# Weights and tokens staged otherwise around the block form of a two-layer network after masked attention

## The chip, the cores and the metric

One core of one Trainium2 chip runs the whole program. The metric is device time in microseconds of one execution; the kernel before was timed in three runs, and one more execution was recorded by the hardware profiler.

## What is computed

Attention over 8 batches, 8 heads, 576 positions and 64 columns, in which scores under the row's maximum less tau are dropped; its output x (4608 tokens by 512) goes through two layers with 2048 hidden columns between them, whose weights come in 64-bit floats.

```python
def _attn_ref(q, k, v, tau):
    scores = scale * np.matmul(q, k.transpose(0, 1, 3, 2))
    thresh = np.max(scores, axis=-1, keepdims=True) - tau
    scores = np.where(scores >= thresh, scores, -1000000000.0)
    ...
    return np.matmul(attn, v)

def _moe_ref(x, w_in, w_out, alpha):
    h = x @ w_in
    g = np.maximum(h, 0.0) + alpha * np.minimum(h, 0.0)
    return g @ w_out
```

## The kernel before

A number goes into TensorE as two parts, a rounded one (`hi`, `xh`, `gh`) and the rest (`lo`, `xl`, `gl`), and each product is three matmuls. The rounded part is made by ScalarE (`split_hi`, line 857), the rest by VectorE or GpSimd (`split_lo`, line 860).

The program has four parts in time. First, attention, 32 pairs of heads, with the two layers for seven of sixteen columns of weights (`fcs1`) worked in between for the first groups of 256 tokens (`groups1`). Second, what is left of that plain form: the loop over `jobs` (line 1094), here four groups of 256 tokens. For each, `first_layer` makes 12 matmuls for each of seven columns of weights, and `second_layer` two accumulators of 21 matmuls each, whose result goes to `part` in memory. The second layer of a group comes after the first one or more columns of the next group. Below, this part is called J. Third, the block form for the eight columns in `fcs2` (and one odd column, `odd`): a 2 by 2 block product is worked with seven products of sums of blocks instead of eight. Its first layer (A) takes the tokens in six blocks `s` of 768, each with four pairs of columns (`NP`), so 24 units `u`, each with seven products (`product_a`, six matmuls of 384 columns) and for two units in four an odd product (`odd_a`, twelve). Fourth, its second layer (B), nine units of 512 tokens, to which `part` is added.

Everything on TensorE, ScalarE, VectorE and GpSimd stands in the order in which it is written; only the order of transfers on SP is left to the compiler. The writing goes by cycles: `cycle()` (line 954) runs the functions that are due, those entered with `first_at_cycle` ahead of those entered with `at_cycle`, and then counts `i` up. In J a cycle is one column of the first layer, or a piece of the second one: `second_layer` calls `cycle()` after its third and its fifth column of weights and at the end of an accumulator, so three for an accumulator and six for a group. In A a cycle is one product, in B a third of one. An instruction that waits holds all that is written behind it on its engine.

Words of weights. The 64-bit words are made into 32-bit floats in seven steps (`Split64`): load, size (two ScalarE instructions), clamp, shift, sign, power, rest, and a sum (`done`). `word_at` (line 844) enters the steps at offsets that `EARLY` or `LATE` give. In J, `first_word` enters one word each `FW` = 5 cycles from cycle `i + 5` on, with its load 4 cycles ahead, into one of two raw tiles `w0`; clamp, shift, sign and power are VectorE's there, rest and `done` GpSimd's. After each second word, `sums_at` makes the seven sums of blocks and splits them. The odd column's word follows (`odd_word`). In A, `late_word` does the same for the second layer's weights, one each 14 cycles; its clamp and rest are GpSimd's, and `done` is VectorE's.

x for the block form. `x_at(s)` (line 1112) loads the four blocks of x for 768 tokens into `xr00`, `xr11`, `xr01`, `xr10`, one tile each, makes the differences and sums 7, 6, 5, 4 (`sub7`, `add6`, `sub5`, `sub4`), some of them in place, and splits the seven operands and the odd one into eleven tiles that turn (`XB`). For `s` = 0 all of it is written around the last second layer of J: load, difference 7, operand 1 and sum 6 ahead of it, the other operands (`others`) behind it and ahead of the first product. For the later blocks it is entered at cycles counted back from the first product that needs it: the load 33 before, difference 7 at 25 before, operand 1's copy at 28 before, and so on.

Accumulators. A has seven banks: X (three buffers), W and Y (two each). Products 1, 7 and 2 begin a bank; 6, 5, 3 and 4 add to one that has been saved in between. `after_a`, entered for the cycle after the product, evicts: ScalarE saves products 1, 7 and 6 as `c` (line 1306), VectorE makes the sums (line 1329), ScalarE copies them (line 1314), VectorE takes the larger with alpha (line 1317), and SP writes them to `gd`.

Of the kernel before, what the change touches and what calls it, by code (L numbers as in the profile page):

```python
# [21 lines left out]
P = 128  # L22
# [3 lines left out]
F1 = 7  # L26
# [54 lines left out]
def tile_masked_attention_moe(  # L81
# [760 lines left out]
    EARLY, LATE = (0, 1, 2, 3, 4, 5, 6), (0, 1, 3, 4, 5, 6, 9)  # L842
# [20 lines left out]
    def fetch_x(t0, n, c, lead, name):  # L863

        st = {"xr": {}}

        def load(k):
            xr = st["xr"][k] = mem.lx.tile([P, G1], F32, tag="xr", name=f"xr{name}_{k}", bufs=NCC)
            t = t0
            while t < t0 + n:  # L870
                b, o = divmod(t, S)
                m = min(S - o, t0 + n - t)
                nc.sync.dma_start(xr[:, t - t0 : t - t0 + m], xs[b][k, :, o : o + m])
                t += m

        def split(k):
            if k == 0:
                st["parts"] = tuple(mem.lx.tile([P, NCC, G1], F32R, tag=t, name=f"{t}{name}", bufs=2) for t in ("xh", "xl"))
            xr, (xh, xl) = st["xr"][k], st["parts"]
            nc.scalar.activation(xh[:, k, :n], xr[:, :n], AF.Copy)  # L880
            nc.gpsimd.tensor_tensor(xl[:, k, :n], xr[:, :n], f(xh[:, k, :n]), op=ALU.subtract)
# [8 lines left out]
    with tc.manual_schedule(engines=ENGINES) if ENGINES else ExitStack():  # L890
# [60 lines left out]
        mem.ws = pool(1, "ws", "left")  # L951
# [15 lines left out]
        def first_word(n, c):  # L967

            pr, r = divmod(n, 2)
            w = Split64(mem.ws, ("w0", 2), mem.ws, ("w1", 2), "vpp", *src_i(fcs2[n]))  # L970

            def done(w):
                if r == 0:
                    w32[pr] = mem.lx.tile([P, 2, DM], F32, tag="w32", name=f"w32_{pr}", bufs=2)
# [6 lines left out]
        def sums_at(c, pr):  # L981
# [5 lines left out]
            def temps():  # L987
                for n in (7, 6):
                    st[n] = mem.ws.tile([P, m], F32, tag=f"sum{n}", name=f"sum{n}_{pr}", bufs=1)
# [28 lines left out]
        def odd_word(io, c, lead):  # L1018
            w = Split64(mem.ws, ("w0", 2), mem.ws, ("w1", 2), "vpp", *(src_i if io == "i" else src_o)(odd))
            decode_at(c, mem.wa, w, odd, io, c - lead, io == "o")  # L1020
# [26 lines left out]
        odd_word("i", c, 4)  # L1047
# [45 lines left out]
        pending = None  # L1093
        for num, job in enumerate(jobs):
            fetch(num + 1)
            final = num == len(jobs) - 1
            for k, j in enumerate(job.todo):
                if k == 0 and num == 1 and pending.begun:
                    cycle()
# [515 lines left out]
```

## Time and profile before

| | us |
|---|---|
| median of 3 runs | 1389.84 (1389.79 to 1391.35) |
| the profiled execution | 1391.04 |
| its span, first to last instruction | 1389.26 |
| TensorE busy | 1314.6 |
| VectorE busy | 1128.8 |
| ScalarE busy | 957.3 |
| GpSimd busy | 795.8 |

The busy times are unions of instructions' spans over the whole program; the span is cut into stretches further down, since what holds TensorE differs from one to the next. A wait is shown as the engine, the tile that it was about to write and the line, and behind the arrow the instruction whose end let it go. Times in the chain of waits are its own pieces; "issue" is time for which the profile shows no wait.

### The profile page before, as it was taken

How to read it: one execution, taken by the hardware profiler on the slowest of the kernel's cores; microseconds unless marked ns; L12 is line 12 of the kernel's file. 1: busy time of each engine (PE TensorE's matmuls, PEld its weight loads, DVE VectorE, ACT ScalarE, POOL GpSimd, SP SyncE). 2: the span in 40 equal slices, each digit the busy share in tenths (PEclk: the TensorE clock that was granted, in tenths of full speed). 3: DMA queues.
4: the chain of work that ended last, by engine and by line, in shares of the span. 5: the costliest groups of instructions: out<-in, count | busy, mean ns of one | idle time of the engine just before them, and what ended most of it. 6: DMA issues, size and time to landing. Idle time of an engine off the chain costs nothing.

```text
span 1389.3 us, 26361 instructions
## 1 busy us (share of the span) xinstructions
PE 1314.6 (95%) x9052; PEld 1227.5 (88%) x9052; DVE 1128.8 (81%) x2134; ACT 957.3 (69%) x2103; POOL 795.8 (57%) x961
## 2 busy tenths in 40 slices
PE   5998899999999999999999999986999999999998
PEld 4556789999999999999999998876999998999998
DVE  6999988888888888898898864883877867878685
ACT  6888888888888888888888853444666666332332
POOL 4786675666666666676676546777877765000000
PEclk9999999999999999999999999998999999999999
DMA  8554634545545545454454313333555536756652
GB/s 250 157 152 111 181 106 125 161 117 141 149 114 152 137 132 140 132 147 122 130 160 126 104 48 116 93 99 120 173 173 173 163 116 215 239 177 188 184 153 90
DMA packets 138005, 200.35 MB, mean 144 GB/s; under 512 B 15792, under 2 KB 83408, under 8 KB 137872
## 3 DMA queue, kind: packets, MB, share of 16 engines
q1 hardware_dynamic: 137872, 198.67, 48.6%
q8 instruction: 72, 1.18, 0.4%
q14 instruction: 61, 0.50, 0.1%
HBM read 106.77 MB, written 49.69 MB: 113 GB/s over the span
## 4 chain that ended last, share of the span: by engine, by line
PE 62%; DVE 12%; DMA 8%; ACT 7%; issue 5%; POOL 5%; SPq 1%; DVEq 0%; ACTq 0%; POOLq 0%
PE av L579 11%; PE s L432 11%; PE acca L254 9%; PE pha L218 9%; PE t L476 7%; PE pX L1256 4%; PE pX L1502 3%; PE pW L1256 2%; DMA pin<-part 2%; DMA out_dram<-pin 2%; DVE gl L861 2%; DVE pin L1524 1%; DVE p L467 1%; DMA xr<-xs 1%; DVE nmx L447 1%
## 5 line engine op out<-in xcount | busy, mean ns | idle before, releaser
L447 DVE TENSOR_REDUCE nmx<-s 128x1 f32<-128x576 f32 x288 | 217.2, 754 | 72.3 <-PE s L432 69.0
L467 DVE SCALAR_TENSOR_TENSOR p<-s,thr,p 128x576 f32<-128x576 f32 x256 | 206.8, 808 | 3.0 <-ACT thr L460 2.6
L455 ACT ACTIVATE p<-s,nmx 128x576 f32<-128x576 f32 x256 | 189.9, 742 | 8.3 <-DVE nmx L447 7.9
L254 PE MATMUL acca<-wo,ga 128*128 128x512 f32 x588 | 186.3, 423 | 1.5 <-issue 0.8
L432 PE MATMUL s<-kh,qst 128*128 128x288 f32 x640 | 141.6, 311 | 34.7 <-DVE p L467 19.5
L218 PE MATMUL pha<-xh,wi 128*128 128x256 f32 x784 | 156.8, 283 | 0.2 <-ACT pra L231 0.2
L476 PE MATMUL t<-ident,p 128*128 128x128 f32 x1024 | 154.8, 274 | 0.0
L432 PEld LDWEIGHTS s<-kh,qst 128*128 128x128 f32 x640 | 100.5, 191 | 59.4 <-issue 26.3
L432 PE MATMUL s<-kl,qst 128*128 128x288 f32 x640 | 133.3, 298 | 0.0
L218 PEld LDWEIGHTS pha<-xh,wi 128*128 128x128 f32 x784 | 127.7, 190 | 4.8 <-ACT pra L231 1.5
L1256 PE MATMUL pX<-xh,wa 128*128 128x384 f32 x384 | 110.3, 345 | 18.2 <-ACT c L1306 10.2
L476 PEld LDWEIGHTS t<-ident,p 128*128 128x128 f32 x1024 | 126.7, 142 | 0.1
L254 PEld LDWEIGHTS acca<-wo,ga 128*128 128x128 f32 x588 | 101.9, 191 | 13.7 <-issue 1.2
L241 POOL TENSOR_TENSOR pta<-pta,pra 128x256 f32<-128x256 f32 x94 | 69.5, 739 | 74.0 <-ACT pra L231 71.3
L218 PE MATMUL pha<-xl,wi 128*128 128x256 f32 x392 | 110.4, 282 | 0.0
L579 PE MATMUL av<-eo,vst 128*128 128x322 f32 (+1 forms) x512 | 107.3, 333 | 0.0
L1502 PE MATMUL pX<-wb,gh 128*128 128x256 f32 x576 | 104.2, 282 | 0.0
L532 DVE TENSOR_TENSOR eo<-t,eo 128x512 fp32r<-128x512 f32 (+1 forms) x168 | 97.4, 592 | 8.2 <-ACT eo L528 8.0
L432 PEld LDWEIGHTS s<-kl,qst 128*128 128x128 f32 x640 | 102.1, 191 | 0.0
L1256 PEld LDWEIGHTS pX<-xh,wa 128*128 128x128 f32 x384 | 71.9, 192 | 21.3 <-ACT c L1306 11.6
L1502 PEld LDWEIGHTS pX<-wb,gh 128*128 128x128 f32 x576 | 89.1, 190 | 0.0
L528 ACT ACTIVATE eo<-t 128x512 fp32r<-128x512 f32 (+1 forms) x168 | 84.7, 521 | 5.3 <-PE t L476 4.4
(246 smaller groups left out, 3907.4 us busy)
## 6 DMA issues: line engine op xcount, KB each, us to landing
gd<-c SPq DMA_DIRECT2D x72, 192.0 KB
gr<-gd SPq DMA_DIRECT2D x24, 512.0 KB
kr<-in_k_dram SPq DMA_DIRECT2D x31, 320.0 KB
rb<-rvd SPq DMA_DIRECT2D x64, 144.0 KB
xs<-xa SPq DMA_DIRECT2D x32, 288.0 KB
pin<-part SPq DMA_DIRECT2D x18, 512.0 KB
out_dram<-pin SPq DMA_DIRECT2D x18, 512.0 KB
vr<-in_v_dram SPq DMA_DIRECT2D x28, 320.0 KB
```

The costliest lines, as they stand in the source:

```text
L218: nc.tensor.matmul(ph[:, :n], w[:, c, :], xx[:, c, :n], start=(c == 0 and ti == 0), stop=(c == NCC - 1 and ti == 2),)
L254: nc.tensor.matmul(acc[:m, :], gg[:, g, o : o + m], w, start=(first and ti == 0), stop=(last and ti == 2))
L432: nc.tensor.matmul(ps[:, h, :288], w, kk[:, a + h * 288 : a + (h + 1) * 288], start=(ki == 0 and i == 0), stop=(ki == 1 and i == n - 1),)
L447: nc.vector.tensor_reduce(self.nmx[:, j : j + 1], self.S[u][0][:, :, :288], axis=AX.XY, op=ALU.max, negate=True)
L455: nc.scalar.activation(pj, ps[:, :, :288], AF.Exp, bias=nmx[:, j : j + 1], scale=1.0)
L467: nc.vector.scalar_tensor_tensor(pj, ps[:, :, :288], thr[:, j : j + 1], pj, op0=ALU.is_ge, op1=ALU.mult, accum_out=self.sm[:, c : c + 1])
L476: nc.tensor.transpose(tb[:, c, :], pt[:, j, j * D + c * P : j * D + (c + 1) * P], ident)
L528: nc.scalar.activation(dst[0], ps, AF.Copy)
L532: nc.vector.tensor_tensor(dst[1], ps, f(dst[0]), op=ALU.subtract)
L579: nc.tensor.matmul(pa[:m, :n], w, x, start=(part == 0 and c == 0), stop=(part == z.parts[-1] and c == NKC))
L1256: nc.tensor.matmul(ph[:, :H1], a, x[:, c], start=(fresh and c == 0 and ti == 0), stop=(c == 1 and ti == 2), skip_group_check=not fresh,)
L1502: nc.tensor.matmul(acc[:, tb * H2 : (tb + 1) * H2], g[:, pr, tb * P : (tb + 1) * P], w, start=(fresh and n == 0 and ti == 0), stop=(n == l ...
```

## The change

It does six things.

1. Words of weights in J go through three raw tiles and three temporary ones in place of two, with the load 8 cycles ahead (not before the present cycle), and begin one cycle earlier. Their tiles lie in the pool `lx`; the late words' tiles lie in `xe`, the odd column's late weights in `br`.
2. x of a group in J is loaded into the tile of its rest and split in place; odd groups lie in `lx`, even ones in `mp1`, one tile pair each.
3. `second_layer` calls `cycle()` after its first column of weights as well: four for an accumulator, eight for a group.
4. x of the block form's first 768 tokens is loaded into a pool of its own (`xr`) as the last group of J begins; products 1 and 7 and sum 6 are written ahead of the last second layer (`some`), the other operands behind it in another order, and more of its rests are VectorE's. Half of each block's raw x has two tiles.
5. Steps of x in A move by a few cycles (load 29 before in place of 33, operand 1's copy 22 before in place of 28), late words come each 15 cycles from `begin + 6`, and their steps are spread wider.
6. Evictions, copies and the larger of two are entered with `first_at_cycle` in place of `at_cycle`.

```diff
-    EARLY, LATE = (0, 1, 2, 3, 4, 5, 6), (0, 1, 3, 4, 5, 6, 9)
+    EARLY, LATE = (0, 1, 2, 3, 4, 5, 6), (0, 1, 4, 7, 9, 10, 13)
...
-    def fetch_x(t0, n, c, lead, name):
+    def fetch_x(t0, n, c, lead, name, home):
...
-                nc.sync.dma_start(xr[:, t - t0 : t - t0 + m], xs[b][k, :, o : o + m])
+                nc.sync.dma_start(xl[:, k, t - t0 : t - t0 + m], xs[b][k, :, o : o + m])
...
-            w = Split64(mem.ws, ("w0", 2), mem.ws, ("w1", 2), "vpp", *src_i(fcs2[n]))
+            w = Split64(mem.lx, ("w0", 3), mem.lx, ("w1", 3), "vpp", *src_i(fcs2[n]))
...
-            word_at(c, w, c - 4, done)
+            word_at(c, w, max(i, c - 8), done)
...
-                job.x = fetch_x(job.t0, job.n, i, 4, job.name)
+                job.x = fetch_x(job.t0, job.n, i, 4, job.name, mem.lx if num % 2 else mem.mp1)
...
-        c = i + 5
+        c = i + 4
...
-        odd_word("i", c, 4)
+        odd_word("i", c, 8)
...
-                    if j in (2, 4):
+                    if j in (0, 2, 4):
                         cycle()
...
-                    r = st[j, k] = mem.xr.tile([P, 2, H1], F32, tag=f"xr{j}{k}", name=f"xr{s}_{j}{k}")
+                    r = st[j, k] = mem.xr.tile([P, 2, H1], F32, tag=f"xr{j}{k}", name=f"xr{s}_{j}{k}", bufs=1 + k)
...
-                home = mem.pa if slot < 7 else mem.xr if slot == 9 else mem.xe
+                home = mem.pa if slot < 7 else mem.xf if slot < 9 else mem.xe
...
-                if first and n in (7, 6, 2):
+                if first and n in (1, 7, 2, 6, 4):
                     split_lo(nc.vector, xl, st[src(n)], xh)
...
+            def some():
+                sub7()
+                hi(1)
+                lo(1)
+                hi(7)
+                lo(7)
+                add6()
+
+            def others(puts):
+                for n in (2, "o", 6, 4, 5, 3):
+                    if n == "o":
+                        hi_odd()
+                    else:
+                        if n == 4:
+                            sub4()
+                        if n == 5:
+                            sub5()
+                        hi(n)
+                    lo(n)
+                    if puts:
+                        puts.pop(0)()
+
+            if first:
+                load()
+                return some, others
-            at_cycle(max(i, need[1] - 33), load)
-            for c, fn in ((-25, sub7), (-21, add6), (-13, sub5), (-11, sub4)):
+            at_cycle(max(i, need[1] - 29), load)
+            for c, fn in ((-24, sub7), (-18, add6), (-11, sub5), (-10, sub4)):
                 at_cycle(need[1] + c, fn)
-            for c, n in zip((-27, -22, -18, -15, -4, -2, 0), USE):
+            for c, n in zip((-21, -19, -14, -12, -4, -2, 0), USE):
                 at_cycle(need[1] + c - 1, hi, n)
                 at_cycle(need[1] + c, lo, n)
...
+            if final:
+                xs0 = x_at(0)
...
         left[2].close()
-        mem.xr = pool(2, "xraw", "left")
-        others = x_at(0)
-        puts = second_layer(jobs[-1], mem.ws)
+        mem.xe = pool(2, "xe", "left")
+        some, others = xs0
+        some()
+        puts = second_layer(jobs[-1], mem.xe)
...
-                at_cycle(i + 1, copy, g, whole)
-                at_cycle(i + 2, larger, g, whole, alpha_sb)
+                first_at_cycle(i + 1, lambda: copy(g, whole))
+                first_at_cycle(i + 2, lambda: larger(g, whole, alpha_sb))
...
-            word_at(c, w, c - 8, done, fc, LATE)
+            word_at(c, w, max(i, c - 8), done, fc, LATE)
...
-            late_word(n, begin + 8 + 14 * n)
-        odd_word("o", begin + 8 + 14 * NJ, 8)
+            late_word(n, begin + 6 + 15 * n)
+        odd_word("o", begin + 6 + 15 * NJ, 8)
...
-            at_cycle(i + 1, after_a if u < NA else after_b, u, prod)
+            first_at_cycle(i + 1, lambda u=u, prod=prod: (after_a if u < NA else after_b)(u, prod))
```

## Rows read from the trace of the kernel before

**Rows 1.** Page, part 1: busy us, share of the span, instructions of TensorE.
```profile
PE 1314.6 (95%) x9052; PEld 1227.5 (88%) x9052; DVE 1128.8 (81%) x2134; ACT 957.3 (69%) x2103; POOL 795.8 (57%) x961
```

**Rows 2.** Busy time by stretch: J, start, A, turn, second layer.
```profile
core 0: us, PE busy (x) PEld busy (x) DVE busy (x) ACT busy (x) POOL busy (x), PEclk, DMA share, GB/s
850.27:945.12 94.85, 85.14 (x506) 75.41 (x505) 70.69 (x122) 42.72 (x99) 73.49 (x79) 0.95 0.35 108
945.12:976.00 30.88, 20.81 (x103) 19.84 (x102) 13.82 (x21) 15.19 (x26) 20.76 (x20) 0.83 0.34 107
976.00:1156.50 180.50, 173.89 (x980) 172.48 (x979) 135.21 (x207) 116.03 (x219) 133.26 (x120) 0.98 0.53 172
1156.50:1176.00 19.50, 16.55 (x98) 15.26 (x97) 14.48 (x24) 12.54 (x31) 12.92 (x14) 1.00 0.39 133
1176.00:1389.30 213.30, 205.82 (x1706) 203.72 (x1704) 162.99 (x179) 68.41 (x73) 1.81 (x2) 1.00 0.55 174
```

**Rows 3.** Stretches within J: two second layers, ten first layers, three first layers.
```profile
860.34:874.08 13.74, 11.43 (x44) 9.00 (x43) 8.15 (x14) 6.09 (x17) 11.89 (x14) 0.88 0.47 141
885.83:895.69 9.86, 9.86 (x44) 7.81 (x43) 7.09 (x14) 4.33 (x11) 7.33 (x9) 1.00 0.19 56
895.69:918.62 22.93, 17.05 (x122) 16.23 (x121) 20.08 (x33) 10.62 (x26) 17.72 (x21) 0.91 0.22 69
929.48:933.74 4.26, 4.26 (x37) 4.26 (x36) 4.26 (x9) 2.94 (x8) 2.36 (x3) 1.00 0.43 137
```

**Rows 4.** TensorE's waits in J: releaser, us in total, times, longest.
```profile
PE phj L218 <- DVE ptj L237: 5.8, 3, 2.5
PE accj L254 <- POOL gj L248: 3.8, 2, 2.3
```

**Rows 5.** TensorE's longest wait in the start.
```profile
PE pX L1256 <- ACT c L1306: 9.1, 2, 7.3
```

**Rows 6.** TensorE's longest wait in A.
```profile
PE pX L1256 <- DVE pZ L1329: 5.6, 3, 2.9
```

**Rows 7.** VectorE in J by group: busy, mean ns, idle before, releaser.
```profile
L236 DVE TENSOR_SCALAR ptj<-phj,alpha_sb 128x256 f32<-128x256 f32 x28 | 13.3, 476 | 3.9 <-POOL gj L248 3.7
L237 DVE SCALAR_TENSOR_TENSOR ptj<-phj,ptj 128x256 f32<-128x256 f32 x28 | 11.9, 424 | 1.0
L143 DVE TENSOR_SCALAR wti<-wti 128x512 f32<-128x512 f32 x9 | 8.4, 928 | 13.8 <-ACT wti L139 13.7
L994 DVE TENSOR_TENSOR sum<-w,sum 128x256 f32<-128x256 f32 x4 | 1.7, 426 | 0.1
```

**Rows 8.** SP's waits in J, the longest in total.
```profile
SPq L129 <- POOL w L975: 24.2, 6, 6.3
```

**Rows 9.** The shift step of words: ns min/median/max.
```profile
L146 DVE TENSOR_SCALAR wti<-wti x16: 416/582/1425, 13.6 to 929.6; 128x512 int32<-128x512 int32 x16
```

**Rows 10.** Chain of waits in the start: start us, us, what.
```profile
946.42 2.69 DVE xl L861 x3
...
956.80 4.01 DMA xr<-xs
...
961.89 1.00 POOL xt L1135
...
962.92 0.84 ACT xh L858
963.76 0.48 ACT c L1306
```

**Rows 11.** Chain of waits in A.
```profile
1029.01 5.54 DMA xr<-xs
...
1037.21 1.89 POOL wto L143
...
1048.33 2.08 PE pX L1256 x12
```

**Rows 12.** VectorE's waits in A for the late words' clamp.
```profile
DVE wto L146 <- POOL wto L143: 7.7, 4, 4.6
```

More of the change, by code (lines that the diff above doesn't have):

```diff
@@ L861, in split_lo @@
         eng.tensor_tensor(dst, src, f(hi), op=ALU.subtract)
-    def fetch_x(t0, n, c, lead, name):
-        st = {"xr": {}}
+    def fetch_x(t0, n, c, lead, name, home):
+        st = {}
         def load(k):
-            xr = st["xr"][k] = mem.lx.tile([P, G1], F32, tag="xr", name=f"xr{name}_{k}", bufs=NCC)
+            if k == 0:
+                st["parts"] = tuple(home.tile([P, NCC, G1], F32R, tag=t, name=f"{t}{name}", bufs=1) for t in ("xh", "xl"))
+            xl = f(st["parts"][1])
             t = t0
@@ L872, in load @@
                 m = min(S - o, t0 + n - t)
-                nc.sync.dma_start(xr[:, t - t0 : t - t0 + m], xs[b][k, :, o : o + m])
+                nc.sync.dma_start(xl[:, k, t - t0 : t - t0 + m], xs[b][k, :, o : o + m])
                 t += m
         def split(k):
[L877 to L881, printed above, removed]
+            xh, xl = st["parts"]
+            nc.scalar.activation(xh[:, k, :n], f(xl[:, k, :n]), AF.Copy)
+            nc.gpsimd.tensor_tensor(xl[:, k, :n], f(xl[:, k, :n]), f(xh[:, k, :n]), op=ALU.subtract)
             if k == NCC - 1:
@@ L950, in tile_masked_attention_moe @@
         mem.wa = pool(0, "wa", "left")
-        mem.ws = pool(1, "ws", "left")
+        mem.xr = pool(1, "xraw", "left")
         mem.lx = pool(2, "lx", "left")
@@ L988, in temps @@
                 for n in (7, 6):
-                    st[n] = mem.ws.tile([P, m], F32, tag=f"sum{n}", name=f"sum{n}_{pr}", bufs=1)
+                    st[n] = mem.lx.tile([P, m], F32, tag=f"sum{n}", name=f"sum{n}_{pr}", bufs=1)
                 st[5], st[3] = blk(1, 0), blk(0, 1)
@@ L1091, in second_layer @@
             return puts
[L1093 to L1099, printed above, removed]
-                    second_layer(pending, mem.mp1)
-                first_layer(job, j)
-                if k == (GB - F1 - 1 if final else 0) and num > 0 and not (num == 1 and pending.begun):
-                    second_layer(pending, mem.mp1)
-            if not final:
-                pending = job
+        start = {}
         xop = {}
@@ L1137, in temp @@
             def temp(n):
-                st[n] = mem.xr.tile([P, 2, H1], F32, tag="xt", name=f"xt{s}_{n}", bufs=2)
+                st[n] = mem.xe.tile([P, 2, H1], F32, tag="xt", name=f"xt{s}_{n}", bufs=2)
                 return st[n]
@@ L1204, in x_at @@
             at_cycle(need[1] - 16, lo, "o")
+        pending = None
+        for num, job in enumerate(jobs):
+            fetch(num + 1)
+            final = num == len(jobs) - 1
+            if final:
+                xs0 = x_at(0)
+            for k, j in enumerate(job.todo):
+                if k == 0 and num == 1 and pending.begun:
+                    cycle()
+                    second_layer(pending, mem.mp1)
+                first_layer(job, j)
+                if k == (GB - F1 - 1 if final else 0) and num > 0 and not (num == 1 and pending.begun):
+                    second_layer(pending, mem.mp1)
+            if not final:
+                pending = job
         left[2].close()
-        mem.xr = pool(2, "xraw", "left")
-        others = x_at(0)
-        puts = second_layer(jobs[-1], mem.ws)
+        mem.xe = pool(2, "xe", "left")
+        some, others = xs0
+        some()
+        puts = second_layer(jobs[-1], mem.xe)
         p1.close()
-        mem.xe = pool(6, "xe", "left")
+        mem.xf = pool(6, "xf", "left")
         mem.br = pool(3, "br", "right")
@@ L1214, in tile_masked_attention_moe @@
         others(puts)
-        start = {}
         steps = []
```

30 lines of the change are left out of this document (11 added, 19 removed).

## Prediction

> **What bounds the kernel now.** I read the page's first part first: TensorE is busy for 95% of the span [rows 1]. That is no proof that it is full, because a matmul's record overlaps the next one's. So I looked next at stretches of time, and compared what TensorE was given with what the same matmuls take where nothing holds them. The reader should see in [rows 2] five stretches: the last four groups of the plain two-layer form (J), the first 31 us of the block form (start), the rest of its first layer (A), the turn to its second layer, and the second layer.
>
> Undisturbed prices: 36 matmuls of 256 columns in 4.26 us and 42 of 512 columns in 9.86 us [rows 3], so 0.118 and 0.235 each; 12 of 384 columns in 2.08 us [rows 11], so 0.173.
> - J holds 4 x 7 x 12 = 336 of the first kind and 4 x 2 x 21 = 168 of the second: 39.7 + 39.4 = 79.1 us, and takes 94.85 [rows 2]. Lost: 15.7.
> - Start: 103 x 0.173 = 17.8 of 30.9. Lost: 13.0, with the granted clock at 0.83.
> - A: 980 x 0.173 = 169.9 of 180.5. Lost: 10.6.
> - Turn: 74 x 0.173 + 24 x 0.118 = 15.6 of 19.5. Lost: 3.9.
>
> The other engines are full in none of them: in J VectorE is busy 70.7 and GpSimd 73.5 of 94.85 us. It is order, not quantity, that costs: each engine takes its instructions in the order written, and what TensorE needs stands behind something that waits.
>
> Who holds it: in J the activation on VectorE (5.8 us) and the rests of the activations on GpSimd (3.8) [rows 4]; at the start ScalarE's eviction `c`, 9.1 us in two waits [rows 5]; in A VectorE's sum in `pZ` [rows 6]. One step further back, in J VectorE waits 13.8 us for words of weights [rows 7], whose loads wait 24.2 us for GpSimd to free one of the two raw tiles [rows 8].
>
> **Part 1, the words of weights in J.** Three raw tiles and a lead of eight cycles: word n takes the tile of word n-3, which is finished at cycle 5(n-3)+6, nine cycles before word n starts; the load at minus eight finds it free. So SP's 24.2 us of waits should go, and of VectorE's 13.8 us all but the first word (the longest, before any word has landed; its load moves one cycle only). Nothing is added: the same loads, the same steps.
>
> What is late next is VectorE itself. Its two activation steps take 13.3 + 11.9 us for 28 columns of weights [rows 7], 0.90 each. The ten groups of word and sum steps (the two rows of [rows 7] with the smallest and largest sums and eight between) add up to 48.1 us over the 46 cycles in which words run, 1.05 a cycle. A second layer now has eight cycles, not six, so the words end some five cycles sooner and nearly fall out of the last second layers, but they meet TensorE more densely. In eight first layers in a row VectorE has 8 x (0.90 + 1.05) = 15.6 us of work against TensorE's 11.4: 4.2 behind. In the second layer after it: 8 x 1.05 = 8.4 against 9.9: 1.5 caught up. In the ten after that: 19.5 against 14.2: 5.3 more. Four accumulators of slack cover 4 x 1.42 = 5.7, and a second layer needs its last activation only after 6 x 0.70 = 4.2 us. So I expect waits of 3.5 us at the first second layer (13.74 us now, 3.9 over the undisturbed 9.86 [rows 3]; GpSimd's queue there holds the same work in nearly the same order), 2 at the second, 1 to 2 in the run of ten first layers (22.93 us now for 14.2 of work [rows 3]), and none later. New loss 7.5 instead of 15.7: gain 8. Bounds: 12 if only the first wait stays, 0 if VectorE and GpSimd are as slow as at their slowest.
>
> On that last bound, a row and a rule. The row: the same shift step L146 took from 416 to 1425 ns [rows 9]. The Trainium skill (Perfetto Trace Analysis, Optimizing Scalar/DVE Operations) says that GpSimd and VectorE share a read port of SBUF, which some VectorE instructions hold alone, so that work moved between these two may not help. By that rule the denser words would lengthen each other, and two rests of x moved from GpSimd to VectorE would bring nothing; the time would be that of rival 1. The spread in the row agrees with it, but does not say by how much.
>
> **Part 2, x of the first tokens, and the start.** Now the chain is [rows 10]: three rests of 0.90 on VectorE in a row at 946.4, after the last second layer; then at 956.8 the load of the second block's x, which waited for the first block's tiles; it lands 4.0 us later; two GpSimd differences; ScalarE's `xh` at 962.9; and only then its eviction `c` at 963.8, for which TensorE stood 7.3 us. With the change the first block's loads are issued before the last group's first layers, into a pool of their own, and products 1 and 7 (difference, two copies, two rests, one sum) are prepared under the last second layer, 9.86 us of TensorE that hides about 2 x 0.84 + 4 x 0.90 = 5.3 us. The second block's x has second tiles for half of it, and its first copy stands eight steps behind the begin instead of two.
>
> What stays: products 2, 6, 4, 5, 3 and the odd one are still written ahead of the first eviction. On ScalarE and VectorE by turns, after the end of the last second layer: one copy of an accumulator, four copies of x (5 x 0.84, counting the first at the nearest row's price), four rests and differences (4 x 0.90), then the eviction 0.48: 8.3 us. TensorE reaches the step that overwrites that bank after three steps and a double one, 5 x 1.04 = 5.2 us. It waits 3.1; with something for a slower clock I take 4. The second block's first tile can be loaded once the first block's last difference is done (about 6 us in), lands 4 us later at 10, and its copy comes with the ninth step, at about 12: no wait. New loss 4 instead of 13.0: gain 9; bounds 6 (one more wait of the 3 us kind) and 12 (no wait at all).
>
> **Part 3, the steps in A.** The chain is [rows 11]: a load of x issued at 1029.0, because its tile was read until then, lands 5.5 us later; GpSimd's difference follows, behind it the late word's clamp, 1.89; behind that VectorE's shift, sign and power, with the evictions behind them; TensorE stands. VectorE waited 7.7 us for the clamp in four places, 4.6 at most [rows 12]. New: every load finds its tile free, 29 steps ahead, and the difference comes 5 x 1.04 = 5.2 us behind it, against a landing of 5.5; the shift stands three cycles behind the clamp, not two, sign, power and rest further apart; evictions are put first in their cycle. Words come every 15 cycles, half a block of 30 steps, so each block has the same pattern. On GpSimd, the difference in two halves of 1.00 [rows 10] plus the clamp of 1.89 is 3.9 us, some 4 cycles, so the shift may wait up to 1.4 us in a block, which VectorE's slack mostly takes. New loss 1.5 of 10.6: gain 9; bounds 3 (the wait comes back in each block at a third of its size) and 10.6.
>
> Third raw tile, homes of tiles, the odd word's weights in another pool: no work added. In the second layer the evictions change place in their cycle, but the rests there fall into another cycle than the sums, so I count 0. The turn's 3.9 lie in steps that the change doesn't touch; what can move there is the order of transfers, which isn't written by hand: 0, with 3 either way.
>
> **Sum.** 8 + 9 + 9 = 26 us. The profiled execution took 1391.04 (span 1389.26 and what lies around it), 1.2 above the median 1389.84; from the median: 1364.
>
> **Rivals.**
> 1. VectorE and GpSimd become the bound of J and the 8 us stay lost: 1372. For it: VectorE's 20.08 of 22.93 us in the run of ten [rows 3], and the spread in [rows 9]. Against: 13.8 us of VectorE's idle time there is plain waiting for words.
> 2. The loads don't come earlier, because SP's order stays as it is: then only the order of evictions and the x of products 1 and 7 help: about 8 us, 1382. For it: SP issues in one queue, and its waits show in [rows 8]. Against: those waits name the tile, which is now free.
> 3. All of the three losses go: 15.7 + 13.0 + 10.6 less 1 or 2, 1352.
> 4. Slower: the words locked to the block's period meet the clamp wait at every one of eight late words. At 4.4 us of TensorE each, near the longest wait of [rows 12], that is 35 instead of 10.6: 24 lost against 17 won in J and at the start, 1397. It decides from (10.6 + 17) / 8 = 3.4 us a word.
>
> **Chances.** Forecast 0.50 (1357 to 1371); rival 1 0.20; rival 2 0.09; rival 3 0.10; within 0.2% (2.8 us, about what a measurement of this kernel can tell from no change) 0.05; rival 4 0.06. Leaving out rival 2, no change and rival 4 (0.20) gives 1351 to 1380. Faster 0.89, same 0.05, slower 0.06.
>
> **What would show it.** J at about 87 us, with no wait of VectorE for word loads after the first; the waits that remain at its first two second layers. At the start one wait of ScalarE's eviction of 3 to 4 us, none of 7. In A no wait of TensorE for `pZ` above 1 us, and the shift's waits under 1.5. Wrong if J stays above 92 us, if the second block's copy still blocks ScalarE, or if one stall of A repeats in each block.

## The result, and the profile of the changed kernel

The changed kernel takes 1375.41 us (median of four, three of them from 1375.05 to 1375.66), beside 1390.59 for the kernel before on the same chip: ratio 0.9889, 95% interval 0.9870 to 0.9909. It is faster by 15 us where 26 were forecast, and nearer to rival 1 (1372) than to the forecast (1364).

The fourth took 1442.12 us at a granted clock of 0.85, is left out of the ratio, and is the one that was profiled with the result, so the profile shown is that of a further execution (1373.14 us, beside 1393.57 for the kernel before). Its windows, in the same stretches as [rows 2] (J, start, A, turn, second layer; columns are time, then busy us of each engine with its instructions, granted clock, DMA share, GB/s):

```profile
core 0: us, PE busy (x) PEld busy (x) DVE busy (x) ACT busy (x) POOL busy (x), PEclk, DMA share, GB/s
850.27:947.22 96.95, 84.96 (x505) 75.28 (x504) 72.12 (x125) 42.28 (x99) 71.27 (x77) 0.95 0.36 117
947.22:969.88 22.66, 19.72 (x104) 19.39 (x103) 13.46 (x19) 14.14 (x24) 15.06 (x14) 0.92 0.43 133
969.88:1141.67 171.79, 170.42 (x981) 170.10 (x981) 133.22 (x208) 117.17 (x219) 138.48 (x124) 1.00 0.55 178
1141.67:1158.52 16.85, 15.79 (x100) 15.45 (x99) 14.07 (x23) 13.13 (x31) 12.38 (x13) 1.00 0.40 135
1158.52:1371.00 212.48, 204.72 (x1701) 202.85 (x1699) 162.78 (x179) 68.48 (x72) 2.33 (x2) 1.00 0.55 174
```

The stretches are cut here at the same matmuls in both traces: J, then 103 matmuls of the block form, then 980, then 98. From the length of each I take the undisturbed prices of the prediction (the turn's 98 matmuls, cut so, are 69 of 384 columns and 29 of 256); what is left is lost. (Cut so, the kernel before loses 13.3, 11.0 and 4.2 in start, A and turn; by the round windows of [rows 2] it was 13.0, 10.6 and 3.9.)

| lost, us | before | forecast | after | gained |
|---|---|---|---|---|
| J | 15.7 | 7.5 | 17.8 | -2.1 |
| start | 13.3 | 4 | 4.8 | 8.5 |
| A | 11.0 | 1.5 | 2.0 | 9.0 |
| turn | 4.2 | 3.9 | 1.5 | 2.7 |

The sum is 18.1; the two profiled executions differ by 1391.04 - 1373.14 = 17.9. So the block form did what was forecast and the turn a little more. J, where 8 us were to be won, got 2 us worse. The rest of this document is about J above all.

TensorE's waits in J, which answer to [rows 4] (releaser, us in total, times, longest):

```profile
PE phj L218 <- DVE ptj L237: 8.3, 4, 3.7
PE accj L254 <- ACT gj L245: 1.9, 1, 1.9
PE accj L254 <- POOL gj L248: 1.6, 2, 1.3
```

It is still VectorE's activation that TensorE waits for, 8.3 us instead of 5.8. The three rows add up to 11.8 of the 17.8 us lost. Most of the rest is matmuls that took longer than their undisturbed price where the granted clock was lower, above all in the eight first layers from 872.33:

```profile
872.33:890.28 17.95, 14.28 (x97) 14.08 (x96) 15.54 (x26) 7.71 (x19) 13.26 (x14) 0.81 0.21 67
```

Undisturbed they take 96 x 0.118 = 11.4 us; TensorE waited 3.7 in them, and the 2.9 that are left go with the clock of 0.81.

VectorE's own waits in J, first in the kernel before, then in the changed one:

```profile
DVE wti L143 <- ACT wti L139: 13.7, 4, 7.7
DVE ptj L236 <- POOL gj L248: 3.7, 3, 2.0
DVE sum L993 <- POOL w L975: 3.2, 2, 2.0
...
DVE w L1006 <- POOL wa L861: 2.0, 2, 1.3
```

```profile
DVE sum L993 <- POOL w L975: 11.4, 4, 4.3
DVE wti L143 <- ACT wti L139: 7.8, 2, 7.3
DVE ptj L236 <- POOL gj L248: 5.3, 4, 2.0
DVE ptj L236 <- PE phj L218: 1.0, 2, 0.5
```

The loads' share fell as forecast, from 13.7 to 7.8, of which 7.3 is the first word's (5.1 of them before J begins, in both kernels). But the waits for GpSimd rose from 3.7 + 3.2 + 2.0 = 8.9 to 11.4 + 5.3 = 16.7. That VectorE's work and its waits fill J says nothing yet, since an engine that takes its instructions in order does one or the other nearly all the time. What says more is for whom it waits: for TensorE's accumulators only 1.0 us in the changed kernel, and in the kernel before no such row stands. VectorE runs behind TensorE in J, so what stands ahead of an activation in its queue can make TensorE wait.

A piece of VectorE's queue (start us, us, line, operation, idle time before it and releaser) shows how TensorE comes to stand. TensorE began eight first layers at 872.3; VectorE's first activation for them comes at 880.85:

```profile
864.57 0.42 DVE L237 SCALAR_TENSOR_TENSOR ptj<-phj,ptj 128x256 f32<-128x256 f32 x1
864.91 0.77 DVE L156 TENSOR_SCALAR wri<-wti 128x512 int32<-128x512 int32 x1
866.10 0.45 DVE L143 TENSOR_SCALAR wti<-wti 128x512 f32<-128x512 f32 x1 [0.42 <-ACT wti L139]
869.56 0.94 DVE L993 TENSOR_TENSOR sum<-w 128x256 f32<-128x256 f32 x1 [3.01 <-POOL w L975]
...
872.70 0.96 DVE L861 TENSOR_TENSOR wa<-sum,wa 128x256 fp32r<-128x256 f32 x1
873.58 0.96 DVE L1005 TENSOR_TENSOR w<-w 128x256 f32<-128x256 f32 x1
874.46 0.96 DVE L1006 TENSOR_TENSOR w<-w,sum 128x256 f32<-128x256 f32 x1
...
877.12 1.26 DVE L143 TENSOR_SCALAR wti<-wti 128x512 f32<-128x512 f32 x1
878.41 0.83 DVE L146 TENSOR_SCALAR wti<-wti 128x512 int32<-128x512 int32 x1
879.27 1.65 DVE L151 SCALAR_TENSOR_TENSOR wti<-wri,wti 128x512 int32<-128x512 int32 x1
880.85 0.47 DVE L236 TENSOR_SCALAR ptj<-phj,alpha_sb 128x256 f32<-128x256 f32 x1
```

Two things are to be seen. A 3.0 us wait for GpSimd's finished word stands ahead of thirteen steps of words. And these steps are long: the same line L1005 that takes 0.96 here takes 0.41 elsewhere. From 869.56 to 880.85 they fill 11.3 us; at the shortest record of each kind (0.42 and 0.68) it would be 6.0.

### The profile page after: what moved, and what is told of

Same layout as the page of the kernel before. It is cut to its first block, busy times and chain, and to the rows that moved or that the text cites. A ratio compares the mean times of both kernels' runs of the same rounds, so it can differ in the third digit from the quotient of the medians.

```text
span 1440.3 us, 26338 instructions
## 1 busy us (share of the span) xinstructions
PE 1393.4 (97%) x9052; PEld 1299.2 (90%) x9052; DVE 1131.6 (79%) x2136; ACT 961.3 (67%) x2103; POOL 793.5 (55%) x957
## 5 line engine op out<-in xcount | busy, mean ns | idle before, releaser
L254 PE MATMUL acca<-wo,ga 128*128 128x512 f32 x588 | 200.2, 449 | 0.1
L432 PE MATMUL s<-kh,qst 128*128 128x288 f32 x640 | 146.9, 321 | 29.4 <-DVE p L467 14.9
L476 PE MATMUL t<-ident,p 128*128 128x128 f32 x1024 | 169.8, 293 | 0.0
L218 PE MATMUL pha<-xh,wi 128*128 128x256 f32 x784 | 164.7, 293 | 0.1
L432 PE MATMUL s<-kl,qst 128*128 128x288 f32 x640 | 139.2, 309 | 0.0
L476 PEld LDWEIGHTS t<-ident,p 128*128 128x128 f32 x1024 | 135.2, 146 | 0.3
L254 PEld LDWEIGHTS acca<-wo,ga 128*128 128x128 f32 x588 | 105.7, 196 | 16.1 <-POOL ga L248 0.5
L579 PE MATMUL av<-eo,vst 128*128 128x322 f32 (+1 forms) x512 | 114.9, 350 | 0.0
L1514 PE MATMUL pX<-wb,gh 128*128 128x256 f32 x576 | 109.2, 291 | 0.0
L858 ACT ACTIVATE gh<-gr 128x1024 fp32r<-128x1024 f32 x45 | 47.6, 1058 | 75.0 <-PE pX L1514 31.6
L579 PEld LDWEIGHTS av<-eo,vst 128*128 128x128 f32 (+1 forms) x512 | 82.7, 187 | 10.3 <-issue 6.9
```

The costliest lines, as they stand in the source:

```text
L218: nc.tensor.matmul(ph[:, :n], w[:, c, :], xx[:, c, :n], start=(c == 0 and ti == 0), stop=(c == NCC - 1 and ti == 2),)
L254: nc.tensor.matmul(acc[:m, :], gg[:, g, o : o + m], w, start=(first and ti == 0), stop=(last and ti == 2))
L432: nc.tensor.matmul(ps[:, h, :288], w, kk[:, a + h * 288 : a + (h + 1) * 288], start=(ki == 0 and i == 0), stop=(ki == 1 and i == n - 1),)
L476: nc.tensor.transpose(tb[:, c, :], pt[:, j, j * D + c * P : j * D + (c + 1) * P], ident)
L579: nc.tensor.matmul(pa[:m, :n], w, x, start=(part == 0 and c == 0), stop=(part == z.parts[-1] and c == NKC))
L1514: nc.tensor.matmul(acc[:, tb * H2 : (tb + 1) * H2], g[:, pr, tb * P : (tb + 1) * P], w, start=(fresh and n == 0 and ti == 0), stop=(n == l ...
```

## The experiments

All edits are made to the changed kernel; the ratio is always against the kernel before. First the numbers of all of them, since the readings below compare them. "Lengthening" is worked out from the records: every VectorE instruction of words and sums in J, less the shortest that its kind takes (0.41 to 0.43 us; 0.68 for the lines L151, L849 and L975). In the changed kernel it is 9 x (1.017 - 0.682) for L151, 9 x (0.750 - 0.427) for L143, and so on for nine groups. Each loss in J is that of one execution, and executions of one kernel differ by up to 6.6 us (words_each_six, 1370.53 to 1377.14), so a difference of 1 to 3 us between two losses doesn't tell two kernels apart.

| kernel | ratio, 95% interval | J lost | VectorE's waits for loads | for GpSimd | lengthening |
|---|---|---|---|---|---|
| before | 1 | 15.7 | 13.7 | 8.9 | 18.9 |
| changed | 0.9889 (0.9870 to 0.9909) | 17.8 | 7.8 | 16.7 | 18.0 |
| sums_later | 0.9877 (0.9856 to 0.9897) | 18.8 | 7.6 | 19.4 | 16.5 |
| six_cycles | 0.9854 (0.9834 to 0.9874) | 16.3 | 9.1 | 16.1 | 17.7 |
| two_tiles | 0.9873 (0.9854 to 0.9891) | 20.5 | 14.7 | 12.0 | 18.3 |
| words_each_six | 0.9870 (0.9846 to 0.9893) | 19.2 | 7.8 | 15.7 | 15.2 |
| pool_light | 0.980, one run (1364.12 of 1391.69 us) | 7.0 | 10.2 | 1.8 | 13.3 |
| vector_light | 0.980, one run (1364.20 of 1391.69 us) | 9.2 | 9.9 | 20.0 | 12.4 |
| rest_on_vector | 0.9858 (0.9839 to 0.9877) | 14.9 | 6.6 | 11.5 | 17.5 |
| words_on_vector | 0.9809 (0.9794 to 0.9825) | 8.7 | 6.7 | 0 | 11.2 |
| rest_back | 0.9837 (0.9818 to 0.9856) | 16.6 | 7.6 | 7.3 | 15.0 |

**The changed kernel once more.** This is the execution shown above.

> The changed kernel as it is, for a trace at the full granted clock: the profile that came with the result shows TensorE at 0.85 of its clock. Forecast by its terms: J 7.5 us over its undisturbed price, the start 4, A 1.5, the turn 3.9; the measured 1375.4 leaves some 11 us of the forecast's 26 to be found in one of these four or in the second layer. Rival 1 expects them in J (15 lost there), rival 4 in A (a stall of the same kind in each block), an unnamed one at the turn.

**The sums later.** Theory 1 puts J's loss down to the hand-over of the finished word from GpSimd's `done` to VectorE's sums.

```diff
-                sums_at(c + 7, pr)
+                sums_at(c + 9, pr)
...
-            at_cycle(c + 2, later_sums)
+            at_cycle(c + 1, later_sums)
             for n in (5, 3):
-                at_cycle(c + 3, hi, n)
-                at_cycle(c + 4, lo, n, nc.gpsimd if n == 5 else nc.vector)
+                at_cycle(c + 1, hi, n)
+                at_cycle(c + 2, lo, n, nc.gpsimd if n == 5 else nc.vector)
```

> The sums of a pair of words in J begin two cycles later (nine after the odd word's size in place of seven) and are packed into three cycles, so that their last reads stay where they are. Theory 1, the handoff: in J the first sum on VectorE stands one cycle behind GpSimd's sum of two halves of a word (done) and waited 11.4 us for it in four places, with the activations that TensorE needs behind it; then that wait falls under 4 us, J's loss falls from 17.8 to 10 to 12 us and the time by 6 to 8, to about 1368. Theory 2, the density: VectorE and GpSimd have too much to do for TensorE's time while words run; then J loses 16 to 19 as before and other waits take the place.

The wait named went down and two others came up in its place:

```profile
DVE ptj L236 <- POOL gj L248: 7.9, 8, 2.0
DVE wti L143 <- ACT wti L139: 7.6, 2, 7.2
DVE w L1006 <- POOL wa L861: 6.1, 3, 2.0
DVE sum L993 <- POOL w L975: 5.4, 2, 4.2
```

J lost 18.8. The single hand-over isn't the cause; theory 1 falls.

**Six cycles for a second layer, and words every six cycles.** Theory 2 is the density of word steps as such: fewer in a second layer, or fewer everywhere.

```diff
-                    if j in (0, 2, 4):
+                    if j in (2, 4):
```

> The second layer of J calls the cycle three times for an accumulator again, not four; the rest of the change stays. Theory 2 (density): words meet TensorE as thinly as before, with their loads early; J's loss falls from 17.8 to 8 to 11 us, time 1366 to 1368. Theory 1 (handoff): the cycles of a second layer get longer again (1.6 us for 1.2), so the wait of the first sum falls by a half at most; J loses 12 to 15, time about 1371. If neither matters, 17 to 18 and 1375.

```diff
-    FW = 5
+    FW = 6
```

> Words of weights in J each six cycles in place of five, so that they take 55 of J's 61 cycles from its first column on. Theory 2 (density): VectorE's 1.05 us of word work for a cycle falls to 0.88, J loses 8 to 11 us, time 1366 to 1369. Theory 1 (handoff): the first sum stands as close behind GpSimd as now, and waits nearly as long; J loses 14 to 16, time 1372 to 1374.

J lost 16.3 and 19.2. With six cycles the loss moved from the eight first layers (6.6 to 2.2) into a later second layer (none to 3.9); with every sixth cycle the last second layer, free before, lost 6.9. Thinning moves the place. Theory 2, which expected a loss of 8 to 11, isn't borne out. Still, with six cycles the median is 1371.90 and the ratio 0.9854, its interval just touching the changed kernel's: the eight cycles may themselves cost some 3 us. TensorE's waits in J were no shorter for it, 5.4 + 4.3 + 2.5 = 12.2 us against 11.8; the granted clock was 0.98 over J where the changed kernel had 0.95.

**Two raw tiles again.** Part 1 undone by itself.

```diff
-            w = Split64(mem.lx, ("w0", 3), mem.lx, ("w1", 3), "vpp", *src_i(fcs2[n]))
+            w = Split64(mem.lx, ("w0", 2), mem.lx, ("w1", 2), "vpp", *src_i(fcs2[n]))
...
-            word_at(c, w, max(i, c - 8), done)
+            word_at(c, w, c - 4, done)
```

(and the same for the odd column's word)

> Words of weights in J go through two raw and two temporary tiles again, loads four cycles ahead; the rest of the change stays. The forecast's part 1 has these loads as the cause of 6 of VectorE's 13.8 us of waits before: then the wait for the words' first step comes back by 4 to 6 us, J loses 20 to 23 and the time is 1377 to 1380. Theory 1 and 2 both hold that the loads were hidden behind the same queues: J loses 17 to 19, time 1374 to 1376.

The waits for loads came back in full, 14.7 us, and the waits for GpSimd fell by 4.7. J lost 2.7 more, in an execution that was the longest of four (1378.22, median 1374.52) and had a granted clock of 0.91 over J; the ratio is the changed kernel's within the intervals. So the third tile does what it says, and it buys almost nothing: VectorE waits elsewhere instead.

**One engine made lighter.** Theory 3: GpSimd's queue is what J waits for. Rival 2': VectorE's own steps.

```diff
         def rest():
+            if fc is None:
+                return
...
-                nc.gpsimd.tensor_tensor(w32[pr][:, r], f(w.t), f(w.low), op=ALU.add)
+                nc.scalar.activation(w32[pr][:, r], f(w.t), AF.Copy)
```

> From the changed kernel, the words of J are lightened on GpSimd: the multiplication of the low part by the power (`rest`, 8 x 1.18 us) is left out, and the addition that finishes a word (`done`, 8 x 1.36 us) is replaced by a plain copy on ScalarE (8 x about 0.8 us). That takes about 20 us off GpSimd's 70 in J; the words' value is not the reference's, since their low part is left out. Theory 3 (GpSimd's in-order queue is what J waits for, first through the finished word, then through the remainder of the activations): J's loss falls from 17.8 to 6 or less, VectorE's wait of the sums for the finished word (11.4) goes, its wait of the activations for GpSimd (5.3) goes too; the time falls by about 10 us. Rival 2' (VectorE's own steps of words are too much for J): little changes, loss 12 or more.

```diff
         for d, step in zip(pace[1:], (w.clamp, w.shift, w.sign, w.power, rest)):
-            at_cycle(c + d, step)
+            if fc is not None or step in (w.clamp, rest):
+                at_cycle(c + d, step)
```

> From the changed kernel, shift, sign and power of the words in J are left out (8 x (0.56 + 1.02 + 0.75) = 18.6 us of VectorE's 71.5 in J); the words' exponents are not decoded, so their value is not the reference's. GpSimd's work stays as it is. Theory 3: J's loss stays at 12 or more, since GpSimd's queue is unchanged. Rival 2' (VectorE's own steps): the loss falls to 6 or less and the time by about 10 us.

Both took some 9 us off the time, so neither theory holds alone. VectorE's waits with the lighter VectorE (its lines stand one further down than in the changed kernel):

```profile
DVE ptj L236 <- POOL gj L248: 10.0, 7, 2.7
DVE wti L143 <- ACT wti L139: 9.9, 3, 7.4
DVE sum L994 <- POOL w L976: 9.4, 4, 5.0
```

Its waits for GpSimd even rose to 20.0 us (these two rows and one of 0.6), and still J lost only 9.2. So a wait of VectorE for GpSimd isn't a loss by itself; it becomes one when it and the work around it make an activation late for TensorE. Work of VectorE and waits for GpSimd are links of one chain, and a shorter link of either kind shortens it.

**One step moved.** If the chain is one, a step moved from the slower engine to the other should help a little.

```diff
-            w = Split64(mem.lx, ("w0", 3), mem.lx, ("w1", 3), "vpp", *src_i(fcs2[n]))
+            w = Split64(mem.lx, ("w0", 3), mem.lx, ("w1", 3), "vvp", *src_i(fcs2[n]))
```

> From the changed kernel, one step of each word in J (the multiplication of the low part, `rest`) moves from GpSimd (8 x 1.18 us) to VectorE (8 x about 0.9 us); everything is computed. Theory 3: J's loss falls from 17.8 to about 10, time 5 to 7 us below the changed kernel's. Rival 2': VectorE, the bound, gets 7 us more, so the loss rises by 3 to 7 and the time with it. If the two engines hold each other up by a shared port: no change.

J's loss fell by 2.8, in the direction of theory 3 and by less than half of what it expected; the interval (0.9839 to 0.9877) overlaps the changed kernel's.

**All steps moved.** Theories 4 and 5 differ here in sign: is it VectorE's amount of work, or the length that each instruction takes beside GpSimd's?

```diff
-            w = Split64(mem.lx, ("w0", 3), mem.lx, ("w1", 3), "vpp", *src_i(fcs2[n]))
+            w = Split64(mem.lx, ("w0", 3), mem.lx, ("w1", 3), "vvp", *src_i(fcs2[n]))
...
-                nc.gpsimd.tensor_tensor(w32[pr][:, r], f(w.t), f(w.low), op=ALU.add)
+                nc.vector.tensor_tensor(w32[pr][:, r], f(w.t), f(w.low), op=ALU.add)
...
-                    at_cycle(c + k + 1, lo, n, nc.gpsimd if n in (1, 2, 4) else nc.vector)
+                    at_cycle(c + k + 1, lo, n, nc.vector)
...
-                at_cycle(c + 4, lo, n, nc.gpsimd if n == 5 else nc.vector)
+                at_cycle(c + 4, lo, n, nc.vector)
```

> From the changed kernel, all steps of J's words and their sums that GpSimd did move to VectorE: the multiplication (8 x 1.18 us on GpSimd), the finishing addition (8 x 1.36), and the four differences per pair (16 x 0.86); 34 us of GpSimd's 70. Everything is computed. Theory 4 (VectorE's queue, its work at the lengths that it has now, is the chain of J): it gains 11 us of waits for the finished word, but takes 8 x (0.92 + 0.95) + 16 x 0.65 = 25 us more work, so J's loss rises from 17.8 to 25 or more and the time by 7 or more. Theory 5 (what costs is that the same VectorE instruction takes 0.41 us alone and 0.95 beside a GpSimd instruction, 18.0 of its 47.1 us of word steps in J): with GpSimd's half gone most word steps take their short time, the added work is 8 x 1.36 + 16 x 0.41 = 17.5, against which 11 of waits and some 10 of the longer durations go: J's loss falls to 12 to 15, time 3 to 6 below the changed kernel's.

Time 1366.16 us (1362.92 to 1366.58), 9 below the changed kernel; J lost 8.7, less than theory 5 gave. This computes everything and is the fastest complete version here. Its J (window, then VectorE's waits):

```profile
850.06:937.92 87.86, 82.03 (x505) 72.42 (x504) 79.26 (x157) 42.20 (x99) 41.39 (x45) 0.98 0.40 129
```

```profile
DVE wti L143 <- ACT wti L139: 6.7, 1, 6.7
DVE xl L861 <- PE accj L254: 1.9, 1, 1.9
DVE ptj L236 <- PE phj L218: 1.6, 3, 0.6
```

VectorE takes 32 instructions more and is busy only 7.1 us longer (79.3 against 72.1), because the lengthening falls from 18.0 to 11.2. Its waits for GpSimd, 16.7 us, are gone. 7.1 - 16.7 = -9.6, and J became shorter by 96.95 - 87.86 = 9.1; but as J is VectorE's busy and idle time together, this is an account of J and not by itself a cause. TensorE's own waits in J fell from 11.8 to 2.9 + 2.3 + 0.5 = 5.7, and the granted clock rose from 0.95 to 0.98. Theory 4, which takes the lengths as given, expected a loss of 25 or more; it falls. Theory 3 doesn't fall by this run: GpSimd's queue is shorter too, 41.4 us busy in place of 71.3.

The lengths themselves, line L1005 in the changed kernel and in this one (times seen, then shortest, median and longest ns):

```profile
L1005 DVE TENSOR_TENSOR w<-w x4: 410/956/958, 873.6 to 931.5; 128x256 f32<-128x256 f32 x4
```

```profile
L1005 DVE TENSOR_TENSOR w<-w x4: 415/416/418, 869.4 to 922.0; 128x256 f32<-128x256 f32 x4
```

In the changed kernel the three records of 955 to 958 ns lie wholly beside a running GpSimd instruction and the one of 410 beside none. In words_on_vector two of the four (at 887.53 and 922.03) run beside one as well and keep 0.42; there GpSimd's began just after VectorE's. The order decides in the other lines too: 34 of the changed kernel's 64 records of words and sums are over 1.2 times the shortest of their kind, and each began while a GpSimd instruction was running; the 18 beside none and the 6 during which one began keep their length.

**One step moved back.** Is VectorE, nearly full in the last kernel, its new bound (theory A), or does each step on GpSimd cost more than it takes off?

```diff
-            w = Split64(mem.lx, ("w0", 3), mem.lx, ("w1", 3), "vvp", *src_i(fcs2[n]))
+            w = Split64(mem.lx, ("w0", 3), mem.lx, ("w1", 3), "vpp", *src_i(fcs2[n]))
```

> As the kernel with the words' steps on VectorE (ratio 0.9809, J's loss 8.7, VectorE busy 79.3 of 86.7 us there), but the multiplication `rest` is on GpSimd again (8 x 1.18 us there, 8 x 0.85 us off VectorE). Theory A (VectorE, nearly full in that kernel, is now the bound of J): J's loss falls to 4 to 6, ratio 0.978 to 0.980. Theory 5 carried on (each GpSimd instruction doubles the VectorE instructions beside it, and VectorE waits for its result again): 6.8 us less work on VectorE, 3 to 5 us back in longer durations, 4 or more in waits for `rest`; loss 10 to 13, ratio 0.982 to 0.984, between the kernel with only `rest` moved (14.9) and that with all moved (8.7).

```profile
DVE wti L143 <- ACT wti L139: 7.6, 1, 7.6
DVE w L975 <- POOL wri L849: 7.3, 5, 2.3
```

The ratio is as theory 5 gave it, 0.9837, and theory A falls. 7.3 us of waits for `rest` and 15.0 - 11.2 = 3.8 of lengthening came back, 11.1 for some 6.8 of work taken off VectorE; the granted clock over J fell from 0.98 to 0.95 as well. The profiled execution lost more (16.6) than the 10 to 13 expected; it was the longest of five (1373.36, median 1371.03), so that loss may be above this kernel's usual one. How much of the 9 us is lengthening and how much hand-over could not be taken apart further: every step that leaves GpSimd ends both.

**The block form: order and spacing.** Two parts of the change undone one at a time.

```diff
-            first_at_cycle(i + 1, lambda u=u, prod=prod: (after_a if u < NA else after_b)(u, prod))
+            at_cycle(i + 1, lambda u=u, prod=prod: (after_a if u < NA else after_b)(u, prod))
```

(and the same at the other places of `after_a` and `after_b`, of `copy` and of `larger`)

> From the changed kernel, only the order within a step of the block form is undone: evictions stand behind the word steps of their cycle again, as before. Theory of part 3 in which the room between load, difference and clamp and the free tiles do it: the loss in the start, A and turn stays at 7 to 9 us (6.96 with the order), none of TensorE's waits in A above 2 us. Theory of order: of the 10.6 us that A lost before, 5 or more come back, and the time rises by as much.

```diff
-    EARLY, LATE = (0, 1, 2, 3, 4, 5, 6), (0, 1, 4, 7, 9, 10, 13)
+    EARLY, LATE = (0, 1, 2, 3, 4, 5, 6), (0, 1, 3, 4, 5, 6, 9)
...
-            late_word(n, begin + 6 + 15 * n)
+            late_word(n, begin + 8 + 14 * n)
...
-            at_cycle(max(i, need[1] - 29), load)
+            at_cycle(max(i, need[1] - 33), load)
```

(and the offsets of the differences and copies of x, as before)

> From the changed kernel, only the layout of the block form's steps is undone (loads of x 33 steps ahead and their differences as before, late words every 14 cycles from 8 with the clamp three cycles and the shift four behind the size step); second tiles and the order of evictions stay. Theory of part 3 (room between load, difference, clamp and shift is what ended A's stalls): 5 us or more of A's 10.6 come back, and VectorE's waits for the late word's clamp with them. Rival (second tiles for x alone did it): A's loss stays within 2 us of the changed kernel's, time too.

| lost, us | start | A | turn | time, ratio |
|---|---|---|---|---|
| before | 13.3 | 11.0 | 4.2 | |
| changed | 4.8 | 2.0 | 1.5 | 0.9889 |
| order_undone | 4.8 | 0.5 | 5.1 | 0.9877 (0.9853 to 0.9902) |
| spacing_undone | 7.8 | 2.9 | 1.6 | 0.9889 (0.9873 to 0.9906) |

TensorE's longest waits, in the turn without the order, and at the start without the spacing:

```profile
PE pX L1268 <- DVE pZ L1341: 2.5, 2, 2.3
```

```profile
PE pX L1268 <- ACT c L1318: 5.4, 1, 5.4
```

The order of evictions isn't what ended A's stalls: without it A lost even less, and only the turn went back to what it had been. The spacing isn't either: without it VectorE waits for the late words' clamp again, but only twice, 2.0 us at the longest, where it was four times and 4.6 [rows 12], and A lost 0.9 more. The start lost 2.9 more, and the turn 3.6 more without the order, but both also move with edits to J alone: the start from 3.2 (words_on_vector) to 6.1 (rest_on_vector), the turn up to 3.8 (words_each_six). Neither edit moves the median measurably.

What is left of the change for A's nine us is above all the second tiles of x. GpSimd's waits for a load of x in A, first before, then with the spacing undone:

```profile
POOL xt L1135 <- DMA xr<-xs: 11.7, 4, 4.2
```

```profile
POOL xl L861 <- DMA xr<-xs: 1.6, 1, 1.6
```

In the changed kernel and without the order there is no such wait. So the loads land in time with the spacing of the kernel before, which speaks for the tiles. It isn't shown, though: a kernel without the second tiles wasn't run, nor one with order and spacing both undone, in which either might have stood in for the other, nor were the new homes of tiles undone.

## Why the prediction was right, and where it was not

**Start: right, by its own steps.** The prediction counted 8.3 us of ScalarE's and VectorE's steps against 5.2 of TensorE's, a wait of 3.1, and took 4 with a slower clock. This answers to [rows 5] (9.1 us in two waits before):

```profile
PE pX L1268 <- ACT c L1318: 2.9, 1, 2.9
```

That group of TensorE's took 3.1 us above its price. TensorE had stood, and in the two groups that follow the granted clock was lower, in the second of them 0.50, the lower of its two levels of 2.4 and 1.2 GHz; they lost another 0.6 and 0.9. In all, with 0.2 in small pieces, 4.8.

**A: right in size, right in its condition, not in its reason.** 1.5 us forecast, 2.0 measured, and none of the waits for `pZ` that [rows 6] has with 5.6 us; TensorE's one wait left in A is another:

```profile
PE pX L1268 <- ACT c L1318: 1.4, 1, 1.4
```

Part 3 named three causes together, free tiles, spacing and order, and leaned on the spacing ("the shift stands three cycles behind the clamp"). The runs leave the first as the likely one, and that not as it was put: "every load finds its tile free" isn't so, since SP still waited 12.7 us in ten places in A for a tile of x, 1.8 at the longest. The loads land in time all the same.

**Turn: forecast as untouched, gained 2.7.** The step that failed is "the turn's 3.9 lie in steps that the change doesn't touch". Its evictions are among those that now stand first in their cycle; without that order the turn lost 5.1. How much of the 2.7 is theirs stays open, since the turn lost 3.8 in words_each_six, which has the order.

**J: the step that failed.** Two statements of part 1 were borne out: the load waits of VectorE fell to little more than the first word's, and TensorE waited for nothing after the ten first layers. SP's waits for a raw tile, which were to go, fell from 24.2 [rows 8] to 13.3. The places came out otherwise: the two second layers lost 2.1 and 3.9 where 3.5 and 2 were forecast, but the eight first layers lost 6.6, where slack was to cover that VectorE is 4.2 behind, and the ten lost 5.6 instead of 1 to 2.

What failed is that sum of VectorE's queue. It counts VectorE's work (1.05 a cycle and 0.90 a column) and lets its waits for GpSimd stand at nothing, though in the kernel before they were 8.9 us; the one clause on it, "GpSimd's queue there holds the same work in nearly the same order", gives them no price. They measured 16.7. In the eight first layers VectorE's first activation came 880.85 - 872.33 = 8.5 us after TensorE had begun, behind a wait of 3.0 for GpSimd's finished word and thirteen steps, most of them lengthened. On an engine that runs behind, a wait that is taken away is not yet a gain: the next thing is reached earlier, and may wait there. The freed 5.9 us of load waits became 7.8 us of waits for GpSimd. Nor has the sum a term for a lower clock, 2.9 us in these eight layers.

Rival 1 has the right outcome, 8 us that stay lost and 1372, and the right row, the spread of the shift step [rows 9]; in two_tiles the load waits were worth 2.7 us in the profiled execution, and nothing that the medians show.

**The rule on the shared port.** The trace shows what the prediction could only suspect: a step of words takes 0.41 us alone and 0.95 where GpSimd's instruction was there first. The Trainium skill (SBUF — State Buffer, Who interferes with whom) says that a VectorE instruction with two inputs in SBUF contends with a GpSimd instruction that reads SBUF. The records of L1005 agree. That denser words lengthen each other, as the prediction drew from its rule, isn't borne out: the lengthening in J was 18.9 us before and 18.0 after. It is a standing cost there, and what the change added is waits. The prediction had cited the Trainium skill (Perfetto Trace Analysis, Optimizing Scalar/DVE Operations) for the rule that work moved between these two engines may not help. Here it depended on how much was moved: all together gave 9 us; one step gave some 3 in the medians, with intervals that overlap.

**The sum.** 26 forecast. 8.5 + 9.0 + 2.7 - 2.1 = 18.1 in the profiled execution, 15 in the medians. The time lies outside the forecast's own 1357 to 1371; the wide range, 1351 to 1380, held it because its bounds took in rival 1. That the turn gave 2.7 us that nobody had forecast, and so brought the time nearer to the forecast, is luck.

## What to carry to other kernels

Before costing an engine's waits at nothing, look for whom it waits: where it hardly ever waits for the engine that it serves, it runs behind, removing one wait may only uncover the next, and what helps is to shorten the whole chain. Where VectorE and GpSimd hand small steps to each other, put a whole chain of steps on one of them rather than sharing it by the step; in this kernel 32 more instructions on VectorE cost it 7.1 us of busy time and ended 16.7 of waits. And when several edits are made for one stall, undo them one at a time: here two, each undone alone, did little or nothing for the stall they were meant for.

## What the runs showed of the hardware

- VectorE's steps from SBUF to SBUF can be more than doubled when they begin beside a running GpSimd instruction (L1005: 0.41 to 0.96 us), and those that read an accumulator are not. VectorE's lines in J of the changed kernel (busy us, mean ns of one):

```profile
L236 DVE TENSOR_SCALAR ptj<-phj,alpha_sb 128x256 f32<-128x256 f32 x28 | 13.4, 479 | 6.6 <-POOL gj L248 5.3 <-PE phj L218 1.0
L237 DVE SCALAR_TENSOR_TENSOR ptj<-phj,ptj 128x256 f32<-128x256 f32 x28 | 11.9, 425 | 1.0
L151 DVE SCALAR_TENSOR_TENSOR wti<-wri,wti 128x512 int32<-128x512 int32 x9 | 9.2, 1017 | 0.1
L143 DVE TENSOR_SCALAR wti<-wti 128x512 f32<-128x512 f32 x9 | 6.7, 750 | 8.0 <-ACT wti L139 7.8
```

The activation's lines L236 and L237 read `phj` in PSUM; their 28 records each stay within 471 to 486 and 424 to 425 ns, whatever GpSimd does. L151 has records from 682 to 1651 ns.
- The lengthening is in the instruction's own record and not in a wait ahead of it, so no view of waits shows it; the spread of one line's durations does. GpSimd's side is touched too, and less in proportion: its line L861, 128x256, took 0.73 us at the shortest and 1.17 at the longest, line L975 1.30 and 1.62 (spans on GpSimd are rough).
- The same addition of two 512-column operands took 1.36 us on GpSimd in the changed kernel and 0.79 on VectorE in words_on_vector.
